# Another table of priorities for the job planner of an attention and gated feed-forward kernel

## The chip, the cores and the metric

The kernel runs on one core of one Trainium2 chip. The metric is the device time of one execution in microseconds. The core has five engines that matter here, each with its own in-order instruction queue: TensorE (PE, with PEld for its weight loads), VectorE (DVE), ScalarE (ACT), GpSimd (POOL), and SyncE (SP), which issues nearly all transfers.

## The reference

Inputs are q, k, v of 8 batches, 8 heads, 576 positions and 64 columns, and three weights of a feed-forward part. In short:

```
q_rot, k_rot = rotate(q), rotate(k)                       # rotary embedding, halves of 32 columns
scores = q_rot @ k_rot.T / sqrt(64);  scores -= max(scores)
attn   = exp(scores);  attn = attn / (sum(attn) + 1e-9)
out    = attn @ v                                         # all heads side by side: x, 8 x 576 x 512
gate   = sigmoid(sum over k of conv_w[k] * x shifted by 4 - k)   # 5 taps along the sequence
result = (gate * (x @ w_val)) @ w_out                     # 512 x 512 weights
```

## The kernel before, in words

Two heads make a pair; there are 32 pairs, and four of them make a batch. The feed-forward part of a batch (two stages of matmuls, with w_val and with w_out) can start when its four pairs are done.

For each pair the kernel loads q and k transposed, and applies the rotary embedding in five steps to each: two multiplications with a table (`mul0`, `mul1`, line 276), their addition (`add`, line 280), a rounded high part (`hi`, line 283, ScalarE) and the rest as a low part (`lo`, line 287). Each product of the scores and of the feed-forward part is three matmuls of high and low parts. Scores go to PSUM in nine tiles of 128x576 (line 304). For each tile VectorE takes the row maximum (`max`, line 310), ScalarE the exponential with the row sum (`exp`, line 323), TensorE transposes it in 128x128 blocks (`t`, line 338), and VectorE or ScalarE copies the transposed blocks to SBUF (`c`, lines 381 and 379). The product with v follows (`pv`, line 393). The row sums are inverted (`rinv`, lines 404 and 405), transposed, written to memory and read back as a broadcast; `norm` (line 432) multiplies. Then ScalarE and GpSimd split x in high and low parts (`xhi`, `xlo`, lines 440 and 444), and five taps (the first on ScalarE, four on VectorE, line 457) and a tanh (`gate`, line 462) make the gate. In the first pair the rotary steps are done in two halves of the sequence.

The weights arrive as 64-bit floats and are decoded on the chip in ten steps per chunk (lines 516 to 530): six on VectorE, three that the table puts on VectorE or GpSimd, and one on ScalarE. w_val has four chunks of 512 columns (`lval`, `dval`) that use two buffers; w_out has eight of 256 columns (`lout`, `dout`) that use one buffer (`wst`), one after the other. conv_w (`taps`, `dtap`) is decoded in the same way, 20 columns wide.

What sets the order is a planner written in Python, which runs while the kernel is built. Every piece of work is a job with an engine, an assumed duration, the data it reads and writes, and a due value: a base (9 per pair, plus the position in it) plus an entry of the table `DUE`. `order` (lines 108 to 182) plays the jobs through a small model of the engines: each engine starts, among the jobs that could start within some 100 ns (`WAIT`) of the earliest, the one with the lowest due value. Buffers are counted too (`BUFS`): two score tiles, three tiles of exponentials, five of x's high and low parts and of the gate, four PSUM banks for the rest. The order found in this way is the order in which instructions stand in each engine's queue; on the chip the queues then run by themselves and wait for one another's semaphores. VectorE jobs with two SBUF inputs and all GpSimd jobs exclude each other in the model (`port`).

`DUE` holds also choices of an engine, as 0 and 1: `e_kmul0` puts that rotary step on VectorE (1) or GpSimd (0), `v1` the copy of transposed block 1 on VectorE or ScalarE, `od2` output copy 2, `eval0` the free steps of a decode. A key ending in `@e` is used for the first five pairs (batch 0 in the feed-forward part) in place of the plain one; a key ending in `_0` or `_1` is the half of the first pair. Keys with more `@e` are not read. Due entries of the first pair's loads and rotary steps have no effect, since their base is below -500:

```
    def opt(key, default=0.0):
        return O.get(key + early, O.get(key, DEFAULT.get(key, default)))

    def at(key, base, *args, **kw):
        plan.add(base + opt(key) * (base > -500), *args, **kw)
```

`run` (lines 184 to 198) issues the jobs in that order. Where the model has TensorE idle in the first 230 us, it fills the gap with transposes of the identity (`fill`, line 331), which compute nothing that is used:

```
    FILL = (3000, 230000, 300, 110, 25)
    n = int((self.start[i] - t - self.FILL[2]) / self.FILL[3]) + (0 if k else self.FILL[4])
```

Of the kernel before, what the change touches and what calls it, by code (L numbers as in the profile page):

```python
# [801 lines left out]
```

## Time and profile before

| what | value |
|---|---|
| three runs | 788.5, 789.59 and 789.95 us; median 789.59 |
| the profiled execution: its time | 784.94 us |
| the profiled execution: span from first to last instruction | 783.2 us |
| TensorE busy | 750.3 us, 96% of the span |
| VectorE busy | 606.9 us, 77% |
| ScalarE busy | 488.6 us, 62% |
| GpSimd busy | 415.9 us, 53% |
| transposes of the identity, line 331 | 395 instructions, 51.7 us, all before 195 us |
| mean granted clock of TensorE | 0.996 |

The busy time of an engine is the time in which at least one of its instructions ran. In a row of groups (`L310 DVE ... x58 | 41.9, 745 | 4.7 <-PE ps_s L304 4.3`) come line, engine, operation, tiles and shapes, the number of instructions, the busy time in us and the mean of one in ns, and the idle time in front of them with what ended it. In a row of the timeline the first two numbers are the start and the length in us. In a table of stretches there is a column of busy time for each engine, with the number of instructions, then the granted clock of TensorE, the share of busy transfer engines and GB/s.

### The profile page before, as it was taken

What the parts mean: (1) busy time and instruction counts of PE and PEld (TensorE: products, weight loads), DVE (VectorE), ACT (ScalarE), POOL (GpSimd) and SP (SyncE); (2) the same over time, 40 slices, a digit from 0 to 9 for tenths busy, and PEclk for the clock granted to TensorE, in tenths of its full rate; (3) what the DMA queues carried; (4) which work ended last, traced back from release to release, by engine and by line L of the source; (5) the groups of instructions that cost most, each with busy time, mean ns of one, the idle gap of its engine ahead of it and who ended that gap; (6) DMA issues with size and microseconds to landing.
All of it is one profiled execution on the core that took longest, in us unless ns stands there. A gap on an engine that the chain in (4) does not pass through costs nothing.

```text
span 783.2 us, 16858 instructions
## 1 busy us (share of the span) xinstructions
PE 750.3 (96%) x6284; PEld 616.0 (79%) x6284; DVE 606.9 (77%) x994; ACT 488.6 (62%) x1155; POOL 415.9 (53%) x300
## 2 busy tenths in 40 slices
PE   8889789899999999999999999999999999999998
PEld 8766666578778887887778787887878788878798
DVE  5898989999877887778687887778687876876640
ACT  2565647556566676766666766766666766766532
...
GB/s 189 158 123 128 82 45 94 127 82 73 90 116 94 94 101 95 108 84 64 116 116 101 89 112 102 102 72 71 109 116 107 91 106 110 114 30 24 33 42 62
DMA packets 92884, 73.81 MB, mean 94 GB/s; under 512 B 60633, under 2 KB 71426, under 8 KB 92802
## 3 DMA queue, kind: packets, MB, share of 16 engines
...
## 4 chain that ended last, share of the span: by engine, by line
PE 67%; DVE 21%; DMA 4%; ACT 4%; issue 3%; SPq 1%; POOL 1%; POOLq 0%; ACTq 0%; DVEq 0%
PE ps_f L480 21%; PE ps_a L393 15%; PE ps_s L304 14%; PE ps_t L338 14%; DVE nm L310 5%; DVE g L457 5%; ACT p L323 2%; DMA kin<-in_k 2%; DVE sums L404 2%; DVE pt L381 1%; PE ps_t L331 1%; DMA qin<-in_q 1%; DVE y L488 1%; DVE k L287 1%; DVE wst L523 1%
## 5 line engine op out<-in xcount | busy, mean ns | idle before, releaser
L323 ACT ACTIVATE p<-ps_s,nm 128x576 f32<-128x576 f32 x288 | 211.9, 739 | 117.2 <-DVE nm L310 114.7
L310 DVE TENSOR_REDUCE nm<-ps_s 128x1 f32<-128x576 f32 x288 | 208.9, 750 | 53.7 <-PE ps_s L304 52.3
L338 PE MATMUL ps_t<-ident,p 128*128 128x128 f32 x1312 | 191.4, 279 | 15.7 <-ACT p L323 9.5
L338 PEld LDWEIGHTS ps_t<-ident,p 128*128 128x128 f32 x1312 | 146.2, 141 | 50.5 <-issue 20.4
L304 PE MATMUL ps_s<-k,q 64*128 64x288 f32 (+1 forms) x1728 | 172.5, 309 | 4.3 <-ACT p L323 3.1
L393 PE MATMUL ps_a<-pt,v 128*64 128x320 f32 (+1 forms) x1280 | 170.5, 411 | 0.0
L304 PEld LDWEIGHTS ps_s<-k,q 64*128 64x128 f32 (+1 forms) x1728 | 135.2, 185 | 33.7 <-issue 18.9
L276 POOL TENSOR_TENSOR qin<-qin,tab_q 128x640 f32<-128x640 f32 x62 | 102.3, 1660 | 95.6 <-DMA qin<-in_q 95.6
L379 ACT COPY pt<-ps_t 128x512 f32<-128x512 f32 (+2 forms) x261 | 118.8, 466 | 27.5 <-PE ps_t L338 24.8
L393 PEld LDWEIGHTS ps_a<-pt,v 128*64 128x64 f32 x1280 | 85.8, 136 | 60.9 <-issue 10.1
L457 DVE SCALAR_TENSOR_TENSOR g<-x,cw,g 128x576 f32<-128x576 f32 (+2 forms) x132 | 118.2, 899 | 1.7 <-ACT g L454 1.4
L480 PE MATMUL ps_f<-y,wout_hi 128*128 128x288 f32 (+2 forms) x512 | 111.1, 304 | 2.4 <-ACT pt L379 2.4
L381 DVE COPY pt<-ps_t 128x512 f32<-128x512 f32 (+1 forms) x155 | 97.0, 629 | 10.3 <-PE ps_t L338 10.2
L287 POOL TENSOR_TENSOR q<-qin,q 128x640 fp32r<-128x640 f32 (+1 forms) x32 | 52.7, 1648 | 69.3 <-ACT q L283 63.9
L480 PEld LDWEIGHTS ps_f<-y,wout_hi 128*128 128x128 f32 x512 | 82.5, 189 | 5.0 <-ACT pt L379 3.5
L444 POOL TENSOR_TENSOR xl<-x,xh 128x576 fp32r<-128x576 f32 (+2 forms) x33 | 45.6, 1383 | 73.1 <-ACT xh L440 59.9
L495 POOL TENSOR_TENSOR y<-y,y 128x288 fp32r<-128x288 f32 (+2 forms) x64 | 54.2, 848 | 54.2 <-ACT y L492 54.1
L480 PE MATMUL ps_f<-xh,wval_hi 128*128 128x288 f32 (+2 forms) x256 | 77.9, 304 | 0.4 <-DVE x L432 0.3
L480 PE MATMUL ps_f<-xl,wval_hi 128*128 128x288 f32 (+2 forms) x256 | 77.2, 302 | 0.0
L480 PE MATMUL ps_f<-y,wout_lo 128*128 128x288 f32 (+2 forms) x256 | 77.1, 301 | 0.0
L480 PE MATMUL ps_f<-xh,wval_lo 128*128 128x288 f32 (+2 forms) x256 | 76.0, 297 | 0.0
L280 POOL TENSOR_TENSOR kin<-kin 128x640 f32<-128x640 f32 (+1 forms) x32 | 49.9, 1558 | 34.9 <-DVE kin L276 34.0
...
## 6 DMA issues: line engine op xcount, KB each, us to landing
...
```

What stands on the lines that cost most here:

```text
L276: eng.tensor_tensor(out=t[:, i, a:b], in0=t[:, i, a:b], in1=tabs[n][:, i, a:b], op=ALU.mult)
L287: eng.tensor_tensor(out=t[:, 1], in0=ins[n][:, 0, a:b], in1=t[:, 0].bitcast(F32), op=ALU.subtract)
L304: T.matmul(out=tiles[h][:, half, 0:288], lhsT=st["q"][rows, x, c * 128:c * 128 + 128], rhs=st["k"][rows, y, k0:k0 + 288], start=(i == 0), ...
L310: V.tensor_reduce(out=st[f"nm{i}"], in_=st[f"s{i}"], axis=AX.XY, op=ALU.max, negate=True)
L323: A.activation(out=pd.rearrange("p (b x) -> p b x", b=2), in_=st[f"s{i}"], func=AF.Exp, bias=st[f"nm{i}"], scale=1.0, accum_out=sums[p % 2 ...
L338: T.transpose(out=bank[0:rows, j * 128:(j + 1) * 128], in_=src, identity=ident)
L379: A.copy(out=dst, in_=src)
L381: V.tensor_copy(out=dst, in_=src)
L393: T.matmul(out=acc[HEAD[h], 0:n], lhsT=st["v"][:, j, h, :], rhs=st[f"pt{g}"][:, at_:at_ + n], start=(j == 0), stop=(j == 4))
L457: V.scalar_tensor_tensor(out=g, in0=x_sb[:, a + k:b + k], scalar=w, in1=g, op0=ALU.mult, op1=ALU.add)
L480: T.matmul(out=acc[:, 0:n], lhsT=wt[w][:, kc, ds], rhs=mv, start=(kc == 0 and i == 0), stop=(kc == NCH - 1 and i == 2))
L495: G.tensor_tensor(out=ffn[b][1][:, dc, lo:hi], in0=ffn[b, "y", dc, lo], in1=ffn[b][0][:, dc, lo:hi].bitcast(F32), op=ALU.subtract)
```

## The change

The table `DUE` is replaced by another one of the same kind; no other line of the kernel differs. The new one comes from a search that scores each order by the planner's model with the VectorE and GpSimd steps of the first pairs lengthened at random. Base due values, durations, buffers and the code that issues the work are the same. The table is one long line; here it is broken up, and cut to the entries that the text speaks of and that are read by the program:

```diff
-DUE = {... 'v1': 1, 'od5': 1, 'od6': 1, 'od7': 0, 'taps': 142.85, 'dtap': 74.98,
+DUE = {... 'v1': 0, 'od5': 0, 'od6': 0, 'od7': 1, 'taps': 25.46, 'dtap': 80.32,
...
-  'e_kmul0_0@e': 0, 'e_kmul1_0@e': 0, 'e_kadd_0@e': 0, 'e_kmul0_1': 0, 'e_qadd_0@e': 1, 'e_qlo_1@e': 0, 'od2': 0, 'od2@e': 1,
+  'e_kmul0_0@e': 1, 'e_kmul1_0@e': 1, 'e_kadd_0@e': 1, 'e_kmul0_1@e': 1, 'e_qadd_0@e': 0, 'e_qlo_1@e': 1, 'od2': 0, 'od2@e': 0,
...
-  'loadk@e': 23.15, 'loadq@e': 40.2, 'loadv@e': 32.18, 'rw@e': 27.89, 'rr@e': 9.21,
+  'loadk@e': -14.49, 'loadq@e': -6.59, 'loadv@e': 48.62, 'rw@e': 37.75, 'rr@e': 75.39,
...
-  'max0@e': 11.58, 'max1@e': 40.75, 'max2@e': 8.26, 'max3@e': 73.76, 'max4@e': 41.67, 'max5@e': 3.82, 'max6@e': 63.05, 'max7@e': 86.75, 'max8@e': 12.05,
+  'max0@e': -2.24, 'max1@e': 13.52, 'max2@e': 6.98, 'max3@e': 52.78, 'max4@e': -26.1, 'max5@e': -12.43, 'max6@e': -33.51, 'max7@e': 66.61, 'max8@e': -6.44,
...
-  'norm0@e': 10.98, 'norm1@e': 92.61, 'tap1@e': 22.52, 'tap2@e': 58.73, 'tap3@e': 5.51, 'tap4@e': 55.46, 'gate@e': 78.32,
+  'norm0@e': 2.93, 'norm1@e': 61.54, 'tap1@e': -1.76, 'tap2@e': 53.53, 'tap3@e': -36.67, 'tap4@e': -17.09, 'gate@e': -46.15,
...
-  'lval0@e': 80.31, 'lval1@e': 85.53, 'lval2@e': 50.21, 'lval3@e': 11.76, 'dval0@e': 72.95, 'dval1@e': 19.78, 'dval2@e': 71.18, 'dval3@e': 84.53,
+  'lval0@e': 134.12, 'lval1@e': 95.33, 'lval2@e': 68.59, 'lval3@e': 29.97, 'dval0@e': 55.73, 'dval1@e': 17.51, 'dval2@e': 70.54, 'dval3@e': 86.59,
...
-  'dout0@e': 23.08, 'dout1@e': 66.95, 'dout2@e': 70.39, 'dout3@e': 72.48, 'dout4@e': 52.71, 'dout5@e': 45.24, 'dout6@e': 0.61, 'dout7@e': 58.78, ...}
+  'dout0@e': -41.19, 'dout1@e': 20.45, 'dout2@e': -46.43, 'dout3@e': 84.16, 'dout4@e': -16.22, 'dout5@e': 6.15, 'dout6@e': -50.42, 'dout7@e': 21.12, ...}
```

Nearly all other due entries differ as well. Outside the first five pairs the engine choices that differ are `v1`, `od5`, `od6` and `od7`.

More of the change, by code (lines that the diff above doesn't have):

```diff
@@ L29 @@
 W = 640
-DUE = {'dtap': 74.98, 'loadk': 48.54, 'loadq': 69.04, 'loadv': 9.94, 'kmul0': -16.36, 'kmul1': 30.91, 'kadd': -78.47, 'qmul0': -85.08, 'qmul1': 82.56, 'qadd': -79.46, 'khi': 101.4, 'klo': 22.63, 'qhi': 81.17, 'qlo': 35.17, 's0': 90.21, 's1': -79.19, 's2': -24.04, 's3': 6.16, 's4': 2.03, 'max0': 10.8, 'max1': -77.65, 'max2': 15.09, 'max3': -6.55, 'max4': -71.65, 'max5': -4.44, 'max6': -63.07, 'max7': -42.21, 'max8': 9.42, 'exp0': -31.5, 'exp1': -29.69, 'exp2': 66.45, 'exp3': 86.44, 'exp4': 5.02, 'exp5': -86.96, 'exp6': 62.59, 'exp7': 58.53, 'exp8': 4.01, 't0': -1.58, 't1': -2.77, 't2': 21.87, 't3': 13.49, 't4': -0.48, 't5': 20.16, 't6': 13.79, 't7': -1.14, 't8': 1.8, 'tm': -83.44, 'th0': 4.91, 'th1': 8.05, 'thm': 8.38, 'cm': -90.06, 'ch0': 6.28, 'ch1': 4.96, 'chm': -84.97, 'c0': 85.46, 'c1': 41.3, 'c2': 66.4, 'c3': 4.01, 'c4': 64.17, 'c5': 33.94, 'c6': 67.47, 'c7': 51.84, 'c8': 2.1, 'vm': 1, 'vh0': 1, 'v1': 1, 'v3': 1, 'v5': 1, 'rinv': -5.21, 'rmm': 4.86, 'rcp': 36.73, 'rw': 10.63, 'rr': 88.11, 'pv00': 8.88, 'pv01': -2.83, 'pv10': 11.87, 'pv11': 9.5, 'norm0': -70.53, 'norm1': 8.55, 'xhi': 9.24, 'xlo': -85.37, 'tap0': 12.19, 'tap1': 35.48, 'tap2': 98.92, 'tap3': 24.38, 'tap4': 80.16, 'gate': 79.66, 'rinvl0': 8.94, 'rmml0': -21.1, 'rcpl0': 88.93, 'rwl0': 49.77, 'rrl0': 84.27, 'norm0l': -76.94, 'xhil0': 82.38, 'xlol0': -86.4, 'tapl0': 77.11, 'gatel0': 74.53, 'rinvl1': 9.36, 'rmml1': 8.32, 'rcpl1': -79.42, 'rwl1': 85.05, 'rrl1': 27.84, 'norm1l': 18.78, 'xhil1': 23.03, 'xlol1': -77.07, 'tapl1': 71.13, 'gatel1': 70.64, 'f00': -2.78, 'f10': 12.84, 'f0l0': -82.01, 'f1l0': 27.94, 'od0': 0, 'f01': 72.91, 'f11': 85.79, 'f0l1': -5.23, 'f1l1': 85.1, 'od1': 0, 'f02': 58.93, 'f12': 68.64, 'f0l2': 74.68, 'f1l2': 94.01, 'od2': 0, 'f03': 74.59, 'f13': 85.67, 'f0l3': -13.25, 'f1l3': 5.1, 'od3': 0, 'f04': 70.17, 'f14': 20.9, 'f0l4': 81.25, 'f1l4': 85.15, 'od4': 1, 'f05': 15.8, 'f15': 96.41, 'f0l5': 34.08, 'f1l5': 35.43, 'od5': 1, 'f06': 85.3, 'f16': 72.55, 'f0l6': 9.24, 'f1l6': 23.18, 'od6': 1, 'f07': -77.02, 'f17': 69.09, 'f0l7': 24.03, 'f1l7': 50.7, 'od7': 0, 'lval0': 21.11, 'dval0': 88.29, 'lval1': 16.29, 'dval1': 92.21, 'lval2': 32.03, 'dval2': 53.45, 'lval3': 72.64, 'dval3': 4.97, 'lout0': 77.72, 'dout0': 4.94, 'lout1': 27.76, 'dout1': 11.22, 'lout2': 30.28, 'dout2': -8.15, 'lout3': 0.03, 'dout3': 7.26, 'lout4': -20.86, 'dout4': 1.4, 'lout5': 72.76, 'dout5': -1.55, 'lout6': 57.28, 'dout6': -8.07, 'lout7': -13.54, 'dout7': 38.24, 'taps': 142.85, 'ltab': 142.61, 'kadd_1': 115.11, 'ltabk_1': 1.97, 'qmul0_0': 39.68, 'ltabq_1': 76.43, 'kmul1_1': 28.81, 'qmul1_0': 128.99, 'klo_1': 65.82, 'e_kmul0_0': 1, 'loadk_1': 7.95, 'qadd_1': 59.55, 'qmul1_1': 23.82, 'e_qmul0_0': 1, 'qmul0_1': 53.74, 'qlo_1': 45.98, 'e_qlo_0': 1, 'qlo_0': 111.98, 'klo_0': 51.25, 'qhi_0': 28.81, 'ltabq_0': -10.85, 'khi_1': 48.54, 'e_kmul0_1': 0, 'loadk_0': -6.68, 'kmul1_0': 98.19, 'kmul0_1': 63.44, 'qhi_1': 120.28, 'kmul0_0': 95.91, 'khi_0': 136.6, 'qadd_0': 129.04, 'loadq_0': 5.57, 'kadd_0': 97.18, 'ltabk_0': -11.32, 'e_kmul1_0': 1, 'loadq_1': 2.89, 'e_qmul1_0': 0, 'e_klo_0': 1, 'e_qadd_1': 1, 'e_klo_1': 1, 'e_kadd_0': 1, 'e_qadd_0': 1, 'e_kmul1_1': 1, 'e_qlo_1': 0, 'qmul1@e': 65.09, 'khi_0@e': 823.23, 'loadq_0@e': 971.53, 'exp3@e': 68.18, 'f15@e': 5.68, 'c4@e': 47.82, 'lval1@e': 85.53, 'qadd@e': 51.56, 'rinv@e': 67.81, 'qmul0_1@e': 808.89, 'dout6@e': 0.61, 'c0@e': -2.83, 'f11@e': 83.18, 'thm@e': -38.35, 'qhi@e': 50.18, 'f13@e': 9.16, 'dout3@e': 72.48, 'max1@e': 40.75, 's0@e': -8.09, 'exp6@e': 66.85, 'qadd_1@e': 808.96, 'ltabk_0@e': 906.6, 'rcp@e': 8.41, 'dout0@e': 23.08, 'tm@e': -16.59, 'pv01@e': 8.16, 'norm0@e': 10.98, 'qmul0@e': 65.04, 'lval3@e': 11.76, 'c7@e': 2.29, 'lval2@e': 50.21, 'max6@e': 63.05, 'loadq_1@e': 979.9, 'xlo@e': 19.63, 's1@e': -15.07, 'e_kmul0@e': 1, 'f07@e': -10.36, 'rw@e': 27.89, 'dval3@e': 84.53, 'f14@e': -32.64, 'f06@e': -85.38, 'xhi@e': 77.45, 'max7@e': 86.75, 'ltabq_1@e': 900.95, 'v1@e': 1, 'tap4@e': 55.46, 'f10@e': 31.15, 'f17@e': 70.53, 't2@e': -9.13, 't7@e': -6.72, 'f02@e': 11.71, 'qadd_0@e': 852.66, 'kmul1_1@e': 706.69, 'e_qlo_1@e': 0, 'norm1@e': 92.61, 'kmul1_0@e': 716.1, 'exp7@e': 63.64, 'ltabq_0@e': 947.35, 'loadk_1@e': 983.74, 'dval2@e': 71.18, 'lout2@e': -25.22, 'loadk_0@e': 935.0, 'loadq@e': 40.2, 'f12@e': 9.99, 'kadd_0@e': 858.68, 'kadd@e': -83.59, 'lout3@e': 48.49, 'tap0@e': 84.39, 'kmul0_0@e': 885.35, 'qmul1_0@e': 865.49, 'qmul0_0@e': 865.14, 'lout1@e': 85.05, 'kadd_1@e': 788.59, 'max5@e': 3.82, 'max8@e': 12.05, 'tap1@e': 22.52, 'exp0@e': 7.79, 'dout7@e': 58.78, 's2@e': -0.43, 'dval1@e': 19.78, 'exp2@e': 76.27, 'c6@e': 22.43, 'pv11@e': 10.08, 't5@e': 2.86, 'exp8@e': 8.01, 'loadk@e': 23.15, 'e_kmul0_0@e': 0, 'khi_1@e': 812.78, 'max2@e': 8.26, 'qhi_0@e': 820.69, 'qlo@e': -92.91, 't6@e': 10.33, 'f03@e': 20.48, 'kmul0@e': 51.79, 'lout5@e': 6.8, 'kmul0_1@e': 866.39, 'chm@e': 42.23, 'qlo_0@e': 833.63, 'kmul1@e': 55.42, 'dout5@e': 45.24, 't3@e': 72.49, 'exp4@e': -25.84, 'ltabk_1@e': 816.6, 'lout6@e': 50.54, 'ch1@e': 8.57, 't4@e': 6.03, 'gate@e': 78.32, 'dout1@e': 66.95, 'klo_0@e': 788.97, 'ch0@e': 6.49, 'max4@e': 41.67, 'lout4@e': 4.85, 'rr@e': 9.21, 'f05@e': 72.07, 'qlo_1@e': 813.43, 'max0@e': 11.58, 'cm@e': 1.23, 't1@e': 18.84, 'e_kadd_0@e': 0, 't0@e': 10.08, 'tap2@e': 58.73, 'e_qmul0_1': 1, 'qhi_1@e': 815.98, 'klo@e': 11.68, 'c3@e': 66.16, 'klo_1@e': 868.21, 'th1@e': 68.44, 'pv00@e': 3.52, 'dout4@e': 52.71, 'f00@e': -91.1, 'qmul1_1@e': 715.36, 'lout7@e': 10.04, 's3@e': -12.07, 'th0@e': 18.27, 'max3@e': 73.76, 's4@e': 11.97, 'c2@e': 70.8, 'f01@e': 65.09, 'lval0@e': 80.31, 'rmm@e': 26.04, 'tap3@e': 5.51, 'c5@e': 72.94, 'pv10@e': 17.3, 'dout2@e': 70.39, 'f04@e': 12.66, 'exp1@e': 19.27, 'exp5@e': 84.35, 'loadv@e': 32.18, 'f16@e': 70.68, 'od5@e': 1, 'dval0@e': 72.95, 'khi@e': 82.43, 'od0@e': 0, 'c1@e': 8.37, 'od7@e': 0, 'lout0@e': 80.38, 'od6@e': 0, 'e_qadd_0@e': 1, 'od3@e': 1, 'od4@e': 0, 'od2@e': 1, 'od1@e': 1, 'e_qmul0_0@e': 1, 'e_kmul0': 0, 'e_kmul1': 1, 'e_kadd': 0, 'e_klo': 1, 'eval0': 1, 'eval1': 1, 'eval2': 0, 'eval3': 1, 'eout0': 1, 'eout1': 0, 'eout2': 0, 'eout3': 1, 'eout4': 1, 'eout5': 1, 'eout6': 1, 'eout7': 1, 'e_kmul1_0@e': 0, 'e_kmul0_0@e@e': 1, 'e_qmul0_0@e@e': 0, 'od2@e@e': 1, 'e_klo@e': 1, 'od0@e@e': 1, 'e_qlo_1@e@e': 1, 'od1@e@e': 1, 'e_kadd_0@e@e': 1, 'v5@e': 0, 'od4@e@e': 1, 'od5@e@e': 1, 'od7@e@e': 0, 'e_kmul0@e@e': 0, 'od6@e@e': 1, 'od3@e@e': 0, 'e_qadd_1@e': 1, 'e_qadd_0@e@e': 1, 'od4@e@e@e': 1, 'e_kmul0@e@e@e': 0, 'e_kmul1_0@e@e': 1, 'e_klo@e@e': 1, 'od5@e@e@e': 0, 'e_qadd_1@e@e': 0, 'od7@e@e@e': 1, 'od2@e@e@e': 0, 'e_qlo_1@e@e@e': 1, 'e_kmul0_0@e@e@e': 0, 'e_kadd_0@e@e@e': 1, 'e_qadd_0@e@e@e': 0, 'od6@e@e@e': 0, 'e_kmul1_1@e': 1, 'e_qmul0_0@e@e@e': 1, 'e_qlo_0@e': 1, 'od0@e@e@e': 1, 'e_qmul1_1': 1, 'e_qmul1_0@e': 1, 'od3@e@e@e': 1}
```

1 line of the change is left out of this document (added).

## The prediction

> **What bounds the kernel now.** I read the page's busy table first, then the busy time by stretches cut at the events found in the timeline, then the same stretches for the warm-up transposes of line 331 alone.
>
> ```profile
> span 783.2 us, 16858 instructions
> PE 750.3 (96%) x6284; PEld 616.0 (79%) x6284; DVE 606.9 (77%) x994; ACT 488.6 (62%) x1155; POOL 415.9 (53%) x300
> ...
> core 0: us, PE busy (x) PEld busy (x) DVE busy (x) ACT busy (x) POOL busy (x), PEclk, DMA share, GB/s
> 0.00:17.00 17.00, 14.38 (x111) 13.94 (x113) 8.20 (x29) 2.71 (x5) 4.21 (x10) 1.00 0.81 200
> 17.00:174.00 157.00, 135.50 (x1142) 105.23 (x1139) 143.83 (x233) 92.94 (x215) 83.54 (x54) 0.98 0.41 105
> 174.00:204.00 30.00, 28.02 (x224) 22.98 (x225) 28.33 (x48) 16.33 (x40) 18.73 (x17) 1.00 0.29 78
> 230.00:760.00 530.00, 527.02 (x4461) 433.55 (x4460) 402.93 (x651) 353.27 (x841) 291.27 (x207) 1.00 0.33 90
> 760.00:783.20 23.20, 19.81 (x146) 19.37 (x144) 3.27 (x7) 6.00 (x14) 4.40 (x6) 1.00 0.15 52
> ```
>
> The same stretches, line 331 only (PE, then PEld):
>
> ```profile
> 0.00:17.00 17.00, 13.64 (x105) 13.41 (x105) 1.00 0.81 200
> 17.00:174.00 157.00, 36.90 (x283) 32.84 (x283) 0.98 0.41 105
> 174.00:204.00 30.00, 1.15 (x7) 0.80 (x7) 1.00 0.29 78
> ```
>
> From 230 to 760 TensorE is busy 527.02 of 530 us: its work there is the time, and no order makes it less; 2.98 us are left to win. Before that TensorE is not the bound. From 17 to 174 it is busy 135.50 us, of which 36.90 are transposes that compute nothing, so its useful work is 98.6 of 157 us, and VectorE is busy 143.83 of 157 (92%). The start is VectorE's: each microsecond that VectorE loses, or gets back, there moves everything behind it by about one microsecond. From 174 to 204 useful TensorE work is 28.02 - 1.15 = 26.87 of 30: 3.1 us are lost.
>
> The timeline shows what opens each stage of the feed-forward part of batch 0.
>
> ```profile
> 172.68 0.68 DVE L530 TENSOR_TENSOR wval_lo<-wst 128x512 fp32r<-128x512 f32 x1
> 173.76 0.41 PE L480 MATMUL ps_f<-xh,wval_hi 128*128 128x288 f32 x1
> 200.47 1.19 POOL L530 TENSOR_TENSOR wout_lo<-wst 128x256 fp32r<-128x256 f32 x1 [0.43 <-DVE wst L523]
> 204.42 0.54 PE L480 MATMUL ps_f<-y,wout_hi 128*128 128x288 f32 x2
> ```
>
> Stage 0 starts 0.4 us after the last quarter of w_val is decoded (172.68 + 0.68 = 173.36), stage 1 starts 2.8 us after the last eighth of w_out (201.66). The weight decode, nearly all VectorE's, competes in this stretch with the attention of the first pairs. Its share is the same window for the tile wst alone:
>
> ```profile
> 0.00:174.00 174.00, 48.04 (x86) 4.89 (x10) 6.48 (x6) 0.98 0.45 115
> 174.00:204.00 30.00, 8.28 (x14) 0.81 (x2) 3.17 (x3) 1.00 0.29 78
> ```
>
> (DVE, ACT, POOL.) 48.04 us of VectorE's time lie before stage 0, and 8.28 us of w_out's decode after it.
>
> **The change part by part.** The table holds priorities, engine choices and nothing else; no job is added or removed. The matmuls stay the same, except the number of line 331's, which the planner works out from its own gaps.
>
> *Prologue of pair 0.* Four rope steps of k (both multiplications and the addition of half 0, the first multiplication of half 1) and the low part of q's half 1 go from GpSimd to VectorE, one addition of q goes the other way. Rows of the timeline:
>
> ```profile
> 11.44 0.87 POOL L276 TENSOR_TENSOR kin<-kin,tab_k 128x320 f32<-128x320 f32 x1 [2.02 <-DMA kin<-in_k]
> 11.48 1.18 DVE L287 TENSOR_TENSOR k<-kin,k 128x320 fp32r<-128x320 f32 x1 [1.32 <-ACT k L283]
> 12.92 0.48 DVE L276 TENSOR_TENSOR kin<-kin,tab_k 128x320 f32<-128x320 f32 x1
> 14.57 0.56 DVE L276 TENSOR_TENSOR qin<-qin,tab_q 128x384 f32<-128x384 f32 x1 [1.17 <-issue]
> 15.05 0.48 DVE L280 TENSOR_TENSOR kin<-kin 128x320 f32<-128x320 f32 x1
> 1.36 13.64 PE L331 MATMUL ps_t<-ident 128*128 128x128 f32 x105 [1.36 <-POOL ident masks.py:199]
> 16.07 0.40 PE L304 MATMUL ps_s<-k,q 64*128 64x288 f32 x2 [1.07 <-ACT k L283]
> ```
>
> The first scores (16.07) wait for k's half 1, whose addition (15.05) stands in VectorE's queue behind q's multiplication, which waited 1.17 us. With k's half 1 wholly on VectorE the addition can stand at 13.40 (12.92 + 0.48) or a little later: up to 15.05 - 13.40 = 1.65 us earlier. TensorE's 105 warm-up transposes end at 15.00, so unless their number falls the scores gain only 16.07 - 15.00 = 1.07. I take -1.1; bounds -1.65 and +2.1. The added VectorE work, four steps at 0.48 and one at some 0.55 (the 384-wide row) less one addition, 2.1 us, lies under waits of its queue (1.32 and 1.17 us, and it stood still before the first rope step); without that cover it costs its own 2.1 us, the upper bound.
>
> *Loads.* conv_w's load moves from priority 93.9 (-49 + 142.85) to -23.5 (-49 + 25.46), just ahead of pair 1's k (9 - 18 - 14.49 = -23.5). For the first five pairs loadk falls by 38, loadq by 47, loadv rises by 16. The small conv_w load is one more issue ahead of k on SP's queue; behind it wait the k and q loads, and GpSimd's rope behind them. Waits of VectorE that this touches:
>
> ```profile
> 32.40 0.18 DVE L516 TENSOR_SCALAR ctmp<-cst 128x20 int32<-128x20 int32 x1 [1.28 <-DMA cst<-in_conv_w]
> ...
> L276 DVE TENSOR_TENSOR kin<-kin,tab_k 128x640 f32<-128x640 f32 x11 | 9.2, 845 | 3.8 <-DMA kin<-in_k 3.8
> ```
>
> 1.28 + 3.8 = 5.1 us is all that loads can give; a load that is early only helps where its buffer is free (one buffer for k, one for q). I take half, -2.5; bounds -5.1 and +2 (a v load late by as much as the mean wait for k, 3.8 / 2 of the two long ones).
>
> *Steps given to ScalarE.* The copy c1 leaves VectorE from pair 5 on, output copy 2 of batch 0 too; outputs 5, 6 leave and 7 joins later.
>
> ```profile
> L381 DVE COPY pt<-ps_t x155: 409/681/693, 22.8 to 746.2; 128x512 f32<-128x512 f32 x123, 128x256 f32<-128x256 f32 x32
> L379 ACT COPY pt<-ps_t x261: 207/577/619, 20.2 to 746.7; 128x512 f32<-128x512 f32 x73, 64x64 f32<-64x64 f32 x32, 128x256 f32<-128x256 f32 x26
> ```
>
> (min/median/max ns.) 27 copies at 0.68, 18 us, leave VectorE, but only those of pairs 5 and 6 fall where VectorE sets the pace: at most 1.4. I take -1.1. Later it is worth nothing: TensorE hides it. ScalarE takes 27 x 0.58 = 16 us more over 530 in which it is busy 353; it has the room.
>
> *Priority of decode against attention.* In the first pairs w_out's decode priorities (dout0 to dout7) go from a mean of 49 to -3, those of w_val stay (62 to 58), the row maxima fall by some 31 (mean 38 to 7), the first half's normalisation by 8. So w_out moves ahead of attention, w_val behind it. What the old order costs is seen once:
>
> ```profile
> 109.49 1.11 PE L338 MATMUL ps_t<-ident,p 128*128 128x128 f32 x4 [3.62 <-DVE x L432]
> 113.36 0.76 DVE L310 TENSOR_REDUCE nm<-ps_s 128x1 f32<-128x576 f32 x1 [1.32 <-PE ps_s L304]
> 108.00:112.00 4.00, 2.51 (x12) 2.52 (x13) 4.00 (x10) 0.83 (x2) 0.00 (x0) 0.50 0.03 7
> ```
>
> TensorE stood 3.62 us for a normalisation queued behind decode steps, its granted clock fell to 0.50, and its slow scores then left VectorE idle for 1.32 us, the only part that a VectorE-bound stretch really pays. I take -1.0 for that hole. Against it stands w_out's decode: if all of what now lies after stage 0 goes before it, stage 0 opens 8.28 us later, and of the 3.1 us lost between 174 and 204 all come back: +5.2. If it only gets done earlier in holes, stage 1 opens without loss: -3.1. I take the middle, +1.0.
>
> Sum: -1.1 - 2.5 - 1.1 - 1.0 + 1.0 = -4.7 us. The profiled execution took 784.94 us (span 783.2 and 1.7 around it), so 780.2 on its scale. The runs' median, 789.59, lies 4.65 above that execution; on its scale 784.9.
>
> The Trainium skill, "TensorE: Matmul & The Clock Gate", section "HAM oscillation — how this bites in real kernels", asks for no TensorE gap above some 3.4 us. The row at 109.49 agrees (3.62 us, then 0.50). By that rule an order with fewer warm-up transposes and longer real gaps would pay more; I carry nothing for it, since VectorE's pace covers it.
>
> **The rivals.**
>
> *Slower: w_out decoded ahead of w_val.* Stage 0 cannot open before VectorE has done w_val. If the remaining 8.28 us of w_out come first, the price is the +5.2 above in place of +1.0, and with the loads and the hole giving nothing (their 3.5 gone) the sum is +3.0 to +5.2: 794. It decides if stage 0 opens after 180. For it: the priorities as counted. Against: w_out has one staging buffer, so its eight chunks cannot be pulled together at will.
>
> *No change.* VectorE's list up to stage 1 stays the same but for a few copies; what is won in one hole opens another: 789.6, within 1.6 us (0.2%, about what a measurement of this kernel tells from no change). That covers the case in which the planner's gain does not exist on the chip.
>
> *A larger gain: collisions of VectorE and GpSimd.* Several VectorE rows are far above their fastest in this stretch:
>
> ```profile
> L457 DVE SCALAR_TENSOR_TENSOR g<-x,cw,g 128x576 f32<-128x576 f32 x17 | 16.9, 998 | 0.0
> L287 DVE TENSOR_TENSOR k<-kin,k 128x640 fp32r<-128x640 f32 x6 | 7.5, 1250 | 0.0
> L404 DVE TENSOR_SCALAR sums<-sums 128x9 f32<-128x9 f32 x6 | 5.0, 838 | 0.2 <-ACT p L323 0.2
> ...
> L404 DVE TENSOR_SCALAR sums<-sums x35: 143/611/1534, 42.3 to 745.9; 128x9 f32<-128x9 f32 x31, 128x2 f32<-128x2 f32 x3, 128x3 f32<-128x3 f32 x1
> L457 DVE SCALAR_TENSOR_TENSOR g<-x,cw,g x132: 474/810/2190, 80.4 to 760.8; 128x576 f32<-128x576 f32 x124, 128x256 f32<-128x256 f32 x4, 128x320 f32<-128x320 f32 x4
> ```
>
> 17 x (0.998 - 0.81) + 6 x (0.838 - 0.143) + 6 x (1.250 - 0.81) = 3.2 + 4.2 + 2.6 = 10 us of lengthening in three groups alone. An order that avoids 8 of these 10, with the decode's +1.0 gone too, gives 784.9 - 9 = 776. Against it: lengthening at random says nothing of which pairs meet.
>
> The Trainium skill, "SBUF — State Buffer", section "Who interferes with whom", says that the second of the two engines to start on the shared ports is blocked fully; the 128x9 step's 1534 ns beside 143 agree. By that rule nothing is gained unless the meeting itself is moved.
>
> *A hole in the steady part.* From pair 5 on the c1 copies wait in ScalarE's queue behind exponentials, and TensorE's transposes behind them. 2.98 us are idle in 530 now; three times that costs 6 us and outweighs the start: 791.
>
> **How the numbers follow.** Forecast -4.7: 0.40. Larger gain: 0.15. No change: 0.15. Slower by w_out: 0.24. Steady part: 0.06. So faster 0.55, same 0.15, slower 0.30. The predicted time is 784.9; its own range is 782 to 788 (the loads anywhere between -5.1 and 0, the prologue between -1.65 and 0). The range for eight in ten reaches below the larger gain by the rest of the loads' term (776 - 2.6) and above no change by +5.2 and the loads' +2: 773 to 797.
>
> **What would show it.** Right: the first scores near 15 us; VectorE's waits for loads before 174 at half; stage 0 of batch 0 before 174 and stage 1 before 200; fewer than 395 instructions on line 331; from 230 to 760 TensorE as full as now. Wrong: stage 0 after 180 (the decode order decides); VectorE's row means of lines 404, 457 and 287 much lower (collisions decide); TensorE below 99% in the steady part.

## The result, and the profile after

The kernel after takes 800.24 us (median; 796.3 to 801.47), the kernel before, timed beside it, 789.05 us (787.69 to 789.95): 1.0135 times as long, 95% interval 1.0094 to 1.0176. The forecast was 784.9 us and faster; the time also lies outside its range of 773 to 797.

The two profiled executions differ by more than the medians: 801.36 us with a span of 799.6 against 784.94 with 783.2, so 16.4 us where the medians differ by 11.2. What follows accounts for the 16.4. Why other executions of the kernel before take some 4 us more than the profiled one is not seen in any trace; of the executions timed beside the experiments most show a somewhat lower mean granted clock of TensorE (27 of 92 have 0.989 and take 788.4 to 793.0 us, the profiled one has 0.996). The profiled execution of the kernel after has 0.987, but from 230 to 760 us the granted clock is 1.00 in both traces, so the clock doesn't explain what is lost there.

The page's busy table of the kernel after:

```profile
span 799.6 us, 16725 instructions
PE 755.2 (94%) x6247; PEld 617.3 (77%) x6247; DVE 624.2 (78%) x964; ACT 505.6 (63%) x1189; POOL 409.7 (51%) x296
```

VectorE issues 30 instructions fewer than before (964 against 994, with the copies that went to ScalarE) and is nevertheless busy 17 us longer. The stretches of the prediction, after (the columns are those of the prediction's table):

```profile
17.00:174.00 157.00, 133.38 (x1085) 102.79 (x1082) 137.41 (x228) 90.59 (x210) 76.83 (x48) 0.95 0.39 101
230.00:760.00 530.00, 519.11 (x4377) 423.08 (x4374) 419.92 (x615) 368.85 (x871) 289.86 (x205) 1.00 0.34 90
```

From 230 to 760 TensorE is busy 519.11 us and not 527.02, with 84 instructions fewer done. VectorE is busy 17 us longer there with 36 instructions fewer: single steps have become longer.

Where the 16.4 us arise is read from one event per pair, the transpose of its row sums (line 409). Counting pairs from 0, these are pairs 10, 14, 18 and 30 before:

```profile
284.61 0.27 PE L409 MATMUL ps_r<-ident,sums 128*128 128x128 f32 x1
371.84 0.27 PE L409 MATMUL ps_r<-ident,sums 128*128 128x128 f32 x1
459.46 0.27 PE L409 MATMUL ps_r<-ident,sums 128*128 128x128 f32 x1
720.09 0.30 PE L409 MATMUL ps_r<-ident,sums 128*128 128x128 f32 x1
```

and after:

```profile
289.92 0.32 PE L409 MATMUL ps_r<-ident,sums 128*128 128x128 f32 x1
379.27 0.33 PE L409 MATMUL ps_r<-ident,sums 128*128 128x128 f32 x1
468.89 0.32 PE L409 MATMUL ps_r<-ident,sums 128*128 128x128 f32 x1
736.42 0.27 PE L409 MATMUL ps_r<-ident,sums 128*128 128x128 f32 x1
```

| stretch | before | after | difference |
|---|---|---|---|
| start to pair 10 | 284.61 | 289.92 | +5.3 |
| pair 10 to pair 30 | 435.48 | 446.50 | +11.0 |
| pair 30 to the end of the span | 63.11 | 63.18 | +0.1 |

One batch of four pairs (pair 14 to pair 18) takes 89.62 us in place of 87.62. So two thirds of the 16.4 us lie in the steady part, which the prediction had put down as fixed.

The groups of VectorE instructions between 300 and 700 us name the step that has grown, line 457, the taps. Before:

```profile
L457 DVE SCALAR_TENSOR_TENSOR g<-x,cw,g 128x576 f32<-128x576 f32 x74 | 65.6, 886 | 0.0
L287 DVE TENSOR_TENSOR k<-kin,k 128x640 fp32r<-128x640 f32 x18 | 14.7, 817 | 0.0
```

After:

```profile
L457 DVE SCALAR_TENSOR_TENSOR g<-x,cw,g 128x576 f32<-128x576 f32 x73 | 106.5, 1459 | 0.5
L287 DVE TENSOR_TENSOR k<-kin,k 128x640 fp32r<-128x640 f32 x18 | 14.6, 812 | 0.0
```

The spread of the taps in the same stretch (minimum, median and maximum in ns), before:

```profile
L457 DVE SCALAR_TENSOR_TENSOR g<-x,cw,g x74: 756/810/2190, 302.4 to 698.3; 128x576 f32<-128x576 f32 x74
```

and after:

```profile
L457 DVE SCALAR_TENSOR_TENSOR g<-x,cw,g x73: 756/1737/2186, 299.3 to 696.7; 128x576 f32<-128x576 f32 x73
```

The median tap takes 1737 ns in place of 810. VectorE also wins something in this stretch: the row sums' step of line 404 falls from 640 to 159 ns on average. But there are 18 of these against 73 taps. The timeline of one such tap in the kernel after, all engines, cut to the chain that follows from it:

```profile
444.05 2.18 DVE L457 SCALAR_TENSOR_TENSOR g<-x,cw,g 128x576 f32<-128x576 f32 x1
444.06 1.55 POOL L287 TENSOR_TENSOR q<-qin,q 128x640 fp32r<-128x640 f32 x1 [2.16 <-ACT q L283]
...
446.15 0.16 DVE L404 TENSOR_SCALAR sums<-sums 128x9 f32<-128x9 f32 x1
...
446.47 0.40 DVE L488 SCALAR_TENSOR_TENSOR y<-g,ps_f 128x288 f32<-128x288 f32 x1
...
446.91 0.43 ACT L492 CAST y<-y 128x288 fp32r<-128x288 f32 x1 [1.16 <-DVE y L488]
...
447.25 0.58 ACT L379 COPY pt<-ps_t 128x512 f32<-128x512 f32 x1
...
447.88 0.40 PE L480 MATMUL ps_f<-xh,wval_hi 128*128 128x288 f32 x1 [0.62 <-ACT pt L379]
```

A tap and GpSimd's low part of q start within 0.01 us of each other. GpSimd takes its usual 1.55 us, the tap 2.18. Behind the tap in VectorE's queue stands the gated product (line 488), behind that in ScalarE's queue a copy of transposed blocks, and TensorE waits 0.62 us for that copy. In the list of TensorE's waits between 300 and 700 this is the larger of two entries; before, they were 1.9 and 0.4 us. The two together grew by 6.0 us, of the some 9 us that these 400 us lost (4.5 batches at 2.0); the rest doesn't show as a wait:

```profile
PE ps_f L480 <- ACT pt L379: 5.0, 8, 0.6
PE ps_s L304 <- ACT p L323: 3.3, 10, 0.6
```

For each tap from 300 to 700 I took the part that lies within an instruction of GpSimd, and summed it by GpSimd's step (us, and the number of meetings):

| GpSimd step | before | after |
|---|---|---|
| low part of q, line 287 | 3.1 (4) | 27.9 (18) |
| multiplications of q, line 276 | 12.0 (16) | 24.1 (23) |
| multiplication of k, line 276 | 0 | 8.5 (8) |
| addition of q, line 280 | 2.2 (4) | 3.3 (5) |
| second step's low part, line 495 | 3.1 (13) | 5.0 (17) |
| sum | 20.4 | 68.9 |

All 18 low parts of q that run in this stretch meet a tap. (The 71.8, 20.9 and 10.2 us in an expectation further down come from merged rows of the timeline, a few of them counted twice.) The planner's model lets such steps exclude each other, so in the plan they do not meet; on the chip the queues run by their own semaphores.

At the start, the events of the prediction, after:

```profile
15.17 0.40 PE L304 MATMUL ps_s<-k,q 64*128 64x288 f32 x2 [1.10 <-ACT k L283]
...
173.46 0.40 PE L480 MATMUL ps_f<-xh,wval_hi 128*128 128x288 f32 x1
...
212.98 0.43 PE L480 MATMUL ps_f<-y,wout_hi 128*128 128x288 f32 x2
```

The first scores come 0.9 us earlier, stage 0 of batch 0 0.3 us earlier, stage 1 8.6 us later.

### The profile page after: what moved, and what is told of

The parts are those of the page before. It is cut to its first block, busy times and chain, and to the rows that moved or that the text cites. A ratio compares the mean times of both kernels' runs of the same rounds, so it can differ in the third digit from the quotient of the medians.

```text
span 799.6 us, 16725 instructions
## 1 busy us (share of the span) xinstructions
PE 755.2 (94%) x6247; PEld 617.3 (77%) x6247; DVE 624.2 (78%) x964; ACT 505.6 (63%) x1189; POOL 409.7 (51%) x296
## 5 line engine op out<-in xcount | busy, mean ns | idle before, releaser
L338 PE MATMUL ps_t<-ident,p 128*128 128x128 f32 x1312 | 188.3, 281 | 18.8 <-ACT p L323 18.5
L304 PE MATMUL ps_s<-k,q 64*128 64x288 f32 (+1 forms) x1728 | 175.5, 312 | 6.4 <-ACT p L323 4.3
L379 ACT COPY pt<-ps_t 128x512 f32<-128x512 f32 (+2 forms) x288 | 133.8, 479 | 67.8 <-PE ps_t L338 65.9
L457 DVE SCALAR_TENSOR_TENSOR g<-x,cw,g 128x576 f32<-128x576 f32 (+2 forms) x132 | 169.8, 1291 | 2.0 <-ACT g L454 1.2
L304 PEld LDWEIGHTS ps_s<-k,q 64*128 64x128 f32 (+1 forms) x1728 | 137.1, 188 | 36.8 <-issue 17.9
L495 POOL TENSOR_TENSOR y<-y,y 128x288 fp32r<-128x288 f32 (+2 forms) x64 | 57.1, 893 | 108.6 <-ACT y L492 102.3
L287 POOL TENSOR_TENSOR q<-qin,q 128x640 fp32r<-128x640 f32 x31 | 49.8, 1607 | 75.1 <-ACT q L283 75.1
L480 PE MATMUL ps_f<-xh,wval_hi 128*128 128x288 f32 (+2 forms) x256 | 79.7, 311 | 6.2 <-ACT pt L379 6.2
L381 DVE COPY pt<-ps_t 128x512 f32<-128x512 f32 (+1 forms) x128 | 76.3, 614 | 6.6 <-PE ps_t L338 6.6
L280 POOL TENSOR_TENSOR kin<-kin 128x640 f32<-128x640 f32 x31 | 50.1, 1617 | 39.9 <-DVE kin L276 30.6
```

Of the source, the lines that this page charges most:

```text
L280: eng.tensor_tensor(out=t[:, 0], in0=t[:, 0], in1=t[:, 1], op=ALU.add)
L304: T.matmul(out=tiles[h][:, half, 0:288], lhsT=st["q"][rows, x, c * 128:c * 128 + 128], rhs=st["k"][rows, y, k0:k0 + 288], start=(i == 0), ...
L338: T.transpose(out=bank[0:rows, j * 128:(j + 1) * 128], in_=src, identity=ident)
L379: A.copy(out=dst, in_=src)
L381: V.tensor_copy(out=dst, in_=src)
L457: V.scalar_tensor_tensor(out=g, in0=x_sb[:, a + k:b + k], scalar=w, in1=g, op0=ALU.mult, op1=ALU.add)
```

## The experiments

The theory: the loss is made of VectorE steps, the taps above all, that run into GpSimd's rotary steps; the order as such is not slower. The rivals: the copy c1 on ScalarE (a choice of engine in the table); the first pairs alone, whose due values differ most; VectorE simply too full.

Two kinds of kernel are used: "new" is the kernel after with one edit, "old" the kernel before with the same edit. Ratios are to the kernel before, timed alongside.

**Tables spliced at pair 10.** Jobs of pairs 0 to 9 take their due values from one table, later ones from the other.

```diff
+        t = FIRST if now[0] < 10 else O
-        return O.get(key + early, O.get(key, DEFAULT.get(key, default)))
+        return t.get(key + early, t.get(key, DEFAULT.get(key, default)))
```

New table first:

> The new table for pairs 0 to 9 and their batches, the old one from pair 10 on. In the two traces the row-sum transpose of pair 10 stands 5.3 us later after the change (289.92 against 284.61) and that of pair 30 16.3 us later (736.42 against 720.09). Theory steady: most of the loss is made from pair 10 on, so this kernel keeps only the start's 5 us: 794, and TensorE is as full from 300 to 700 as before (over 99%). Rival start: the loss is the decode order of the first pairs and the rest follows from it: 800.

Measured: 796.18 us, 1.0087 (1.006 to 1.0114). Old table first:

> The old table for pairs 0 to 9, the new one from pair 10 on. Theory steady: 11 us above the kernel before, 800, with a batch every 89.6 us in place of 87.6. Rival start: within 2 us of the kernel before, 789 to 791.

Measured: 843.95 us, 1.0703 (1.0665 to 1.0742). The spliced plan is neither order. With the new table first, pair 10 comes at 296.00 us (284.61 before, 289.92 after), and pairs 10 to 30 take 437.40 us (435.48 before). TensorE is busy 97.83 of 100 us from 300 to 400, then 298.44 of 300, over 99% together. That is what the theory of a steady loss expected for the later pairs, but the time lies between the two expectations, since the first pairs are slower than in either kernel. With the old table first, the plan falls into a third pattern:

```profile
350.00:690.00 340.00, 312.71 (x2531) 252.19 (x2529) 223.27 (x349) 214.98 (x505) 175.14 (x124) 0.97 0.31 82
```

TensorE is busy 312.71 of 340 us there, less than in either kernel, and the time fits neither expectation. Where the loss lies can't be read from spliced tables, so the pair decides nothing.

**The copy c1.** The order is held; only the engine on which c1 is issued from pair 5 on is turned round in each kernel.

```diff
-  ... t_copy, p, key, V if va else A, ...
+  out_va = 1 if key == "1" and p >= 5 else va      # 0 in the old order
+  ... t_copy, p, key, V if out_va else A, ...
```

> The new order as it stands, but from pair 5 on the copy c1 is issued on VectorE at its place in the order, as in the kernel before; the planner does not see it. Theory copy: ScalarE's queue with one copy more per pair holds the score and bank hand-over up; giving it back wins most of the steady 11 us: 790. Rival order: where the other steps stand is the cause, the copy is not; within 3 us of the new kernel (797 to 803), or slower, since VectorE has 18 us more.

> The old order as it stands, with the copy c1 issued on ScalarE from pair 5 on. Theory copy: 8 to 11 us slower than the kernel before, 797 to 800. Rival order: within 3 us of the kernel before, 787 to 792.

Measured: new order with c1 back on VectorE 805.92 us, 1.0211 (1.0181 to 1.0241); old order with c1 on ScalarE 789.02 us, 0.9999 (0.998 to 1.0018). The new choice costs nothing in the old order, and giving it back in the new one makes it about 6 us slower still. The copy is not the cause.

**GpSimd's rotary steps shortened.** Each of GpSimd's rotary steps works on 64 of 640 columns, in one pair of kernels from pair 10 on, in another from pair 2 on; order and engines held.

```diff
+        if eng is G and p >= 10:      # or p >= 2
+            b = 64
```

> The new order as it stands; from pair 10 on GpSimd's rotary steps do 64 of their 640 columns, so the rotary embedding of these pairs is left out in most columns. In the new trace the taps on VectorE (line 457) take 1.46 us on average from 300 to 700 against 0.89 in the old one, each long one beside a GpSimd step. Theory collisions: with short GpSimd steps they return to 0.8 to 0.9, a batch takes 87.6 us in place of 89.6 and the whole 789 to 792. Rival hand-over: the wait of the feed-forward matmul for ScalarE's copy (5.0 us of idle in 400) is a matter of the order on ScalarE and TensorE; 797 to 801.

> The same cut in the old order, as the control. Theory collisions: TensorE is already over 99% busy there, so 787 to 790. Rival hand-over: the same. If this kernel gains as much as the one with the new order, the cut itself gives the time and not the end of collisions.

> The same cut from pair 2 on in the new order. Theory collisions for the start too: VectorE's queue loses its 1.5 to 2 us steps before 200, and the kernel comes within 3 us of the old order with the same cut. Rival w_out chain: the decode of w_out ends later in the new order for a reason in the order (stage 1 of batch 0 at 213.0 against 204.4), so some 5 us or more stay between the two.

> The same cut from pair 2 on in the old order. Theory collisions: 775 to 784, since 10 us of lengthening in three groups of VectorE rows before 174 go. Rival: the start is bound by the number of VectorE steps and not by their lengthening; 785 to 790.

Measured: from pair 10, new 784.22 us, 0.9933 (0.9912 to 0.9953), and old 785.06 us, 0.9949 (0.9925 to 0.9973). From pair 2, new 754.3 us, 0.9556 (0.9523 to 0.9589), and old 760.46 us, 0.9636 (0.9593 to 0.9679). With the late cut the new order wins 16 us and the old one 4, and they come out equal; with the early cut the new order is 6 us ahead. In its trace stage 1 of batch 0 starts at 184.68 us, in the old order's at 187.93, so it is no longer the later one. All four expectations missed: the first, the second and the fourth kernel are 5, 2 and 15 us faster than the collision theory had them, and with the early cut the two orders are not within 3 us of each other. GpSimd's rotary steps cost more than I had counted, in the start of both orders above all. Still, the new order's lag is gone in both pairs: GpSimd's rotary work carries the whole difference. This doesn't tell yet whether by occupying GpSimd, or by what it reads.

**GpSimd occupied, but only writing.** From pair 2 on, each of GpSimd's rotary steps is two memsets of 576 columns and then the step on 64 columns.

```diff
+        if eng is G and p >= 2:
+            for _ in range(2):
+                G.memset(t[:, i, 64:b], 0.0)
+            b = 64
```

> The new order as it stands; from pair 2 on each rotary step of GpSimd is two memsets over 576 columns and then the step on 64 columns, so that GpSimd is occupied for about as long but reads SBUF for a short time only. The rotary embedding is left out in most columns. Theory collisions between two readers: most of the 46 us that the short steps gave come back, 755 to 775. Rival length: GpSimd's occupation itself is what the start and the steady part wait for, 790 to 802.

> The same in the old order, the control. Theory collisions: 760 to 778, and not faster than the new order with the same edit. Rival length: 783 to 790.

Measured: new 756.39 us, 0.9589 (0.9541 to 0.9636); old 761.98 us, 0.9671 (0.9624 to 0.9717), both as the collision theory expected and some 2 us above the short steps. In the new order with writes, the same place in the order as above, GpSimd and VectorE:

```profile
410.93 1.22 POOL L296 MEMSET q<- 128x576 f32 x2 [1.43 <-PE ps_s L316]
...
411.65 0.81 DVE L469 SCALAR_TENSOR_TENSOR g<-x,cw,g 128x576 f32<-128x576 f32 x1
```

The spread of the taps in this kernel from 300 to 700 (line 457 is line 469 here):

```profile
L469 DVE SCALAR_TENSOR_TENSOR g<-x,cw,g x76: 757/810/893, 302.5 to 694.4; 128x576 f32<-128x576 f32 x76
```

GpSimd is busy nearly as long as in the kernel after (209.70 of these 400 us against 226.23), and the taps lie 31.9 us beside it, but none takes more than 893 ns. A GpSimd step that only writes does not lengthen a tap. The Trainium skill, "SBUF — State Buffer", section "Who interferes with whom", says just that: a VectorE instruction with two SBUF inputs contends with a GpSimd instruction that reads SBUF, not with one that only writes it. The traces agree, with 2.18 us beside the reading step and 0.81 beside the writing one.

**Taps with one operand.** GpSimd's steps are whole; the four taps of VectorE are row maxima over the same 576 columns, one SBUF input each.

```diff
-            V.scalar_tensor_tensor(out=g, in0=x_sb[:, a + k:b + k], scalar=w, in1=g, op0=ALU.mult, op1=ALU.add)
+            V.tensor_reduce(out=state[p]["g"][:, a:a + 1], in_=x_sb[:, a + k:b + k], axis=AX.X, op=ALU.max)
```

> The new order as it stands; the four taps on VectorE are replaced by a maximum over the same 576 columns, which reads one SBUF operand and takes about as long (0.75 against 0.81 us); the convolution is left out. GpSimd's steps keep their length. Theory collisions: the steady part returns to 86.2 to 87.6 us a batch, the whole to 786 to 791. Rival length: what the cut GpSimd steps gave was their length, not the end of collisions; 797 to 802 here.

> The same replacement in the old order, the control. Theory collisions: 782 to 788, since the old order pays less for its taps (17 of them 0.19 us each before 174, and 87.6 against 86.2 us a batch). Rival length: 788 to 790.

Measured: new 768.02 us, 0.9733 (0.9679 to 0.9788); old 778.45 us, 0.987 (0.9821 to 0.9919). The new order wins 32 us, the old one 11, and the new one is then 10 us ahead. Both are faster than either of their expectations: the taps cost more than I had counted, before pair 10 too (table below). The spread of the replaced taps in the new order, 300 to 700:

```profile
L457 DVE TENSOR_REDUCE g<-x x72: 694/744/754, 312.0 to 687.9; 128x1 f32<-128x576 f32 x72
```

All 18 low parts of q still meet one of these steps (13.2 us side by side), and none of the 72 is longer than 754 ns. For the taps it takes both: two operands, and a GpSimd step that reads. The same section of the Trainium skill says that this reduction never contends on this chip. The 694 to 754 ns agree.

These kernels leave work out, and so give no price for a whole kernel. The last six leave nothing out: they move GpSimd's rotary steps to VectorE, from pair 5 on, in the order as it is.

**k's steps moved.**

```diff
-                        arg += (eng, a, b)
+                        arg += (V if (n, key) == ("k", "add") and p >= 5 else eng, a, b)
```

The second kernel has `n == "k" and p >= 5` there; the third is the old order with the first edit and c1 on ScalarE.

> The kernel after, order held, with the addition of k's rotary step issued on VectorE in place of GpSimd from pair 5 on. Nothing is left out. By the collision theory this takes one of six GpSimd steps a pair away (1.55 us of GpSimd time) and adds 0.81 us to VectorE, which has about 20 of 100 us free in the steady part: VectorE's taps are lengthened less and the time falls to between 790 and 797. By the rival that VectorE is simply too full in the new order, the added 0.81 us for each of 31 pairs makes it slower: 803 to 810.

> As the run before this one, with all of k's rotary steps (both multiplications, the addition and the low part) on VectorE from pair 5 on. Nothing is left out. Collision theory: two of six GpSimd steps a pair gone, 1.6 us more for VectorE a pair: 784 to 795, and lower than with the addition alone as long as VectorE stays under 95 of 100 us. Rival: slower with each step moved, 808 or more.

> The kernel before, order held, with k's addition on VectorE from pair 5 on and the copy c1 on ScalarE instead (which alone gave 789.02). Nothing is left out. The steady part stands at TensorE's own pace but for about 1 us a batch, so collision theory leaves at most 4 us: 785 to 789. If VectorE's fullness counts: 790 or more.

Measured: the addition alone 797.92 us, 1.0111 (1.0081 to 1.0142); all of k's steps 800.75 us, 1.0145 (1.0108 to 1.0182); old order 786.15 us, 0.9956 (0.9933 to 0.9978). The old order came as expected (785 to 789). My expectation missed in both new kernels: 2 us and nothing, where 3 to 16 were expected. (The edit covers 27 pairs, 5 to 31, and not the 31 of the expectation.) The taps are still at 1423 and 1447 ns, and the overlap, worked out as above, has gone only from 68.9 to 64.3 and 67.1 us: the taps meet q's steps, and I had taken away k's. GpSimd's mean load is not what counts (it fell by a quarter, to 171.86 of 400 us, in the second). The rival is not borne out either: VectorE has 24 us more to do in these 400 us (346.18 against 321.82) and the time is the same.

**q's steps moved.** The same edit with `(n, key) == ("q", "lo")`, with `n == "q"`, and `n == "q"` in the old order.

> The kernel after, order held, with the low part of q (GpSimd's line 287) on VectorE from pair 5 on; nothing is left out. In the trace of after, from 300 to 700, the taps lie 71.8 us beside GpSimd steps (20.9 in before), 27.9 of them beside just this step (18 of 18), and only 10.2 beside k's steps, which is why moving k's gave 2 us and 0. Collision theory: the taps' mean falls from 1459 to some 1075 ns (27.9 us over 73), and more than half of the 16 us comes back: 787 to 793. Rival (VectorE too full, any step moved to it costs): 800 to 808.

> As the run before this one, with all four rotary steps of q on VectorE from pair 5 on (3.3 us more for VectorE a pair, 5 of 6 of the meeting steps gone); nothing is left out. Collision theory: taps below 1000 ns; the steady part is TensorE's if VectorE stays below 95 of 100 us: 780 to 790; if the q steps, long, at their place in VectorE's queue hold up row maxima behind them, 790 to 800. Rival (VectorE too full): 810 or more.

> The control to the last run: the kernel before, its order and its c1 copies held, with all four rotary steps of q on VectorE from pair 5 on; nothing is left out. If the new order is the better one once taps and q's steps do not meet (it was 6 to 10 us ahead in the runs that left work out), this comes out 6 to 10 us above 780.45: 785 to 790. If the two orders are then equal: 778 to 783, and the gain is that of moving q alone.

Measured: the low part alone 787.61 us, 0.9973 (0.9948 to 0.9998), within the 787 to 793 expected; all four steps 780.45 us, 0.9878 (0.9842 to 0.9914), within 780 to 790; the old order 790.06 us, 1.0005 (0.9984 to 1.0025), at the upper end of 785 to 790. The groups from 300 to 700 of the new order with only the low part moved:

```profile
L457 DVE SCALAR_TENSOR_TENSOR g<-x,cw,g 128x576 f32<-128x576 f32 x73 | 76.4, 1047 | 0.5
L287 DVE TENSOR_TENSOR q<-qin,q 128x640 fp32r<-128x640 f32 x18 | 14.7, 819 | 0.0
```

VectorE does the 18 low parts in 14.7 us and has 30.1 us less to do for the taps (106.5 - 76.4); 27.9 were expected from the overlap. The stretch 300 to 700 of the new order with all of q's steps moved, and of the old one:

```profile
300.00:700.00 400.00, 399.73 (x3394) 328.02 (x3394) 344.69 (x547) 287.21 (x677) 114.32 (x91) 1.00 0.37 97
```

```profile
300.00:700.00 400.00, 394.73 (x3359) 324.37 (x3358) 354.30 (x563) 273.02 (x646) 122.27 (x91) 1.00 0.36 97
```

In the new order TensorE is full again (399.73 of 400) although VectorE has more to do than in the kernel after. This whole kernel beats both, by 1.2% against before. In the old order the taps are short as well (799 ns), but VectorE is busy 354.30 us and TensorE loses 5.3 us to waits for exponentials. That kernel keeps c1 on VectorE, as the old table has it; how much of the 10 us between the two is due to that flag and how much to the order wasn't taken apart. Nor is it known whether VectorE's fullness counts in the old order, where the same move gained nothing.

The times of the pairs of kernels, in us:

| edit | old order | new order | new less old |
|---|---|---|---|
| none | 789.05 | 800.24 | +11.2 |
| rotary steps on 64 columns from pair 10 | 785.06 | 784.22 | -0.8 |
| the same from pair 2 | 760.46 | 754.30 | -6.2 |
| the same, GpSimd kept busy with writes | 761.98 | 756.39 | -5.6 |
| taps with one operand | 778.45 | 768.02 | -10.4 |
| q's rotary steps on VectorE from pair 5 | 790.06 | 780.45 | -9.6 |

Where the two orders differ is read from the row-sum transposes again (us; one profiled execution each, so a us or two mean little):

| edit | start to pair 10, old | new | pairs 10 to 30, old | new |
|---|---|---|---|---|
| none | 284.61 | 289.92 | 435.48 | 446.50 |
| rotary steps on 64 columns from pair 10 | 285.06 | 286.95 | 430.19 | 430.67 |
| the same from pair 2 | 268.08 | 259.23 | 430.46 | 430.68 |
| the same, GpSimd kept busy with writes | 265.96 | 262.41 | 430.48 | 430.64 |
| taps with one operand | 284.10 | 271.65 | 430.20 | 432.97 |
| q's rotary steps on VectorE from pair 5 | 284.02 | 281.50 | 437.08 | 434.13 |

With GpSimd's rotary steps short, or writing, the steady part is the same in both orders. With taps of one operand, the new order's start is 12 us shorter than the old one's, while in the whole kernels it is 5 us longer: the new table did make a better start, and the waiting taps took more than all of it.

## Why the prediction was wrong

**The step that failed: the steady part was taken for a fixed time.** "From 230 to 760 TensorE is busy 527.02 of 530 us: its work there is the time, and no order makes it less." An order can make it more, and that is the step that failed: the sum gave this stretch 0, and it cost 11.0 of the 16.4 us, because under the new order the taps meet GpSimd's reading steps (68.9 us of overlap from 300 to 700 in place of 20.4) and TensorE waits behind them. A stretch whose bound engine is 99% busy has little to win from a new order and much to lose, and the table is used for all 32 pairs, not for the first ones. That no order makes it less, and that 2.98 us are left, was a little off too: busy is not the same as unhindered. Without the meetings the 20 pairs from 10 to 30 take 430.2 us in the old order as well, 5.3 less than in the kernel before. The rival that put a hole there had the right place and sign, but 0.06 as its chance, 6 us as its price and the wrong mechanism: the copies behind exponentials in ScalarE's queue cost nothing in the old order (789.02), and undoing them made the new one slower (805.92).

**Collisions were counted as something to win only.** The prediction quoted taps of up to 2190 ns and read from them 10 us that an order might avoid, with the reservation that lengthening at random says nothing of which pairs meet. The same reservation meant that a new order might meet more, and the trace of before had the bounds for it: a tap takes 0.81 us at its median and 2.19 at most. Between 300 and 700 the 74 taps took 65.6 us, 6 above 74 x 0.81 = 60 and 96 below 74 x 2.19 = 162; before stood near its lower end, and a new order had far more to lose than to win. That was to be read before the result. In the start it was the same: the forecast was a gain of 4.7 us there, with one-operand taps the new order's start is 12 us ahead, and with the real taps it is behind. Only a part of it gets through: the taps grew by 41 us in these 400 us, some 9 us a batch, and a batch by 2.0 us. What decides that part was not taken apart.

**Priority of decode against attention (+1.0 booked; bounds -3.1 and +5.2).** Stage 0 at 173.46 against 173.76: nothing lost, so the rival "w_out decoded ahead of w_val" fell too, by its own condition (after 180). Stage 1 at 212.98 against 204.42: worse than the upper bound, and the other way round than argued, since w_out came later and not earlier. ScalarE's step of the decode (line 528) runs once per chunk; its rows for w_out up to 110 us before, and from 110 us on after:

```profile
L528 ACT CAST wout_hi<-wst x4: 400/406/408, 20.7 to 105.4; 128x256 fp32r<-128x256 f32 x4
```

```profile
L528 ACT CAST wout_hi<-wst x5: 397/402/408, 127.8 to 209.4; 128x256 fp32r<-128x256 f32 x5
```

The fourth chunk passes it at 105.4 us before and at 127.8 after, and the last at 197.8 and 209.4. Averaging the eight priorities of the decode is the likely error: with one staging buffer the chunks go one after the other, so the highest due value would set the pace and not the mean, and these highest values have risen (dout3 84 where the highest was 72; of the loads, 140 where it was 85). That it is these entries is argued from the rows and was not tried alone. In the kernels with short GpSimd steps from pair 2, the new order still has 34.3 us from stage 0 to stage 1 and the old one 28.1 (39.5 and 30.7 in the whole kernels), yet its pair 10 comes 8.9 us earlier. So a late stage 1 by itself doesn't account for the loss of the start.

**Prologue (-1.1).** Right: the first scores came at 15.17 (from 16.07), behind 95 warm-up transposes instead of 105. The 0.9 us were lost again by pair 10. The 5.3 us there are one execution's figure: in the two kernels whose GpSimd steps are cut from pair 10 on only, so that their starts are nearly those of before and after, pair 10 comes at 285.06 and 286.95 us, 1.9 apart.

**Loads (-2.5).** Right in its size, not in its worth. VectorE's waits for loads from 17 to 174 fell from 5.1 to 3.1 us (conv_w's is gone). But its waits for scores rose from 4.3 to 11.5 us in the same stretch, as VectorE's waits from 17 to 174 have it after:

```profile
DVE nm L310 <- PE ps_s L304: 11.5, 11, 2.0
DVE kin L276 <- DMA kin<-in_k: 3.1, 2, 2.1
```

and before:

```profile
DVE nm L310 <- PE ps_s L304: 4.3, 7, 1.3
```

VectorE stood behind other engines more often, and a shorter wait for a load did not become time.

**Copies to ScalarE (-1.1, and nothing later).** No effect could be measured in the old order, as said for the steady part. In the new order they are worth about 6 us (805.92 with them undone), which the prediction did not see since it had VectorE with room there.

**The hole (-1.0).** The stop of 3.62 us at 109 us is gone, but there are two like it: 3.52 us in front of 115.40, behind two taps (1.44 and 2.09 us) and a decode step (1.78 us) that GpSimd's steps lengthen, and 3.44 us in front of 166.87. The second one in the timeline of after (VectorE, GpSimd, TensorE), beside one another:

```profile
161.60 1.78 DVE L522 TENSOR_SCALAR wst<-wst 128x512 int32<-128x512 int32 x1
163.30 1.75 DVE L518 SCALAR_TENSOR_TENSOR wst<-wst 128x256 int32<-128x256 int32 x1
164.97 1.50 DVE L404 TENSOR_SCALAR sums<-sums 128x9 f32<-128x9 f32 x1
...
161.40 3.37 POOL L276 TENSOR_TENSOR qin<-qin,tab_q 128x640 f32<-128x640 f32 x2
164.85 1.59 POOL L280 TENSOR_TENSOR qin<-qin 128x640 f32<-128x640 f32 x1
...
166.87 0.45 PE L409 MATMUL ps_r<-ident,sums 128*128 128x128 f32 x1 [3.44 <-DVE wst L519]
```

The table of stretches for 164 to 168 us:

```profile
164.00:168.00 4.00, 1.13 (x6) 1.17 (x7) 3.96 (x7) 0.00 (x0) 2.37 (x2) 0.77 0.00 0
```

Three VectorE steps in a row, each beside a GpSimd step; TensorE stands still for 3.44 us and its granted clock falls to 0.77. From 17 to 174 the clock is 0.95 (0.98 before); line 331 issues 358 transposes of the identity in place of 395.

**What would show it.** Of the signs named, three came as for the forecast (first scores near 15, stage 0 before 174, fewer than 395 instructions on line 331); the waits for loads fell by 39%, not by half; stage 1 came not before 200. The sign "TensorE below 99% in the steady part" decided: 519.11 of 530 is 97.9%. The row means of lines 404 and 287 did fall a little between 17 and 230 (670 to 554, 1105 to 1012 ns), as the larger gain had it; the taps' rose from 1060 to 1247.
